# Routed layer: results scattered through three views of the output, and one gather issued earlier

## The chip, the cores and the metric

One core of one Trainium2 chip. The metric is the time of one execution on the device in microseconds (us). TensorE is called PE below, VectorE DVE, ScalarE ACT, GpSimd POOL; SP is the queue from which most loads are issued. Each engine runs its own instructions in order and waits on semaphores for the others.

## The reference

Three layers follow one another on 1152 tokens of width 512:

```python
x = attention(q, k, v)                    # 2 x 8 heads, 576 tokens, rotary positions, softmax
x = softplus(x @ w_in) @ w_out            # 512 -> 2048 -> 512
do = (x @ w_skip) > 0                     # routed layer from here
out = x.copy()
xc = x[do]
logits = xc @ w_gate                      # 8 experts
e = argmax(logits); p = softmax(logits)[e]
for each expert j: y[e == j] = p * (relu(xc[e == j] @ w1[j]) @ w2[j])   # 512 -> 1024 -> 512
out[do] = xc + y
```

The change lies in the routed layer alone.

## The kernel before

Attention and the second layer take the first part of the span. As the second layer's results come, they are written twice: to a scratch tensor in DRAM (`x2d`, a row of 512 values, a gate and a token number) and to the output, because a token that no expert takes keeps its row. That is the copy at L1489 (`out_dram<-x`, ten transfers of SP).

The routed layer then works on tiles of 128 tokens of one expert. Tile 0 is worked off in `passage`, tiles 1 to 6 in the loop of `tiles` (`range(1, FULL)`, `FULL = 7`); two "small" tiles for the remainders of several experts are woven in (`SMALL`). Tiles beyond that exist only inside conditionals, which this input doesn't enter. In `passage` PE, DVE, ACT and SP issue in the order of the text; in `tiles` all engines do, POOL too.

What a tile T needs, in order:

- `fetch(T)` (L983): POOL gathers the tile's 128 rows from `x2d` into `xg` with an indirect transfer. `small_fetch` (L1185) does it for a small tile. There are five `xg` buffers for tiles 1 to 6.
- `rows(T)` (L997): PE turns `xg` in four transposes into `xgt`; `copies` (L1010 to L1012): ACT and DVE split the result into a high and a low part.
- `split_w`: ACT rounds a chunk of weights (`ws<-raw`, L963) and DVE subtracts it for the low part (L970); 42 of each in the layer.
- `hidden_mm` (L637, `mh`), `relu`, `turn` (L1050 to L1053, `ht`, `hT`), `result_mm` (L637, `y`).
- `finish(T)`: DVE makes the row numbers `si` (L1077) and the results `yo` (L1082), and POOL writes the 128 rows to their places in the output with an indirect transfer (L1083, a scatter). `small_finish` does it for a small tile (L1166). Rows that are only padding have a number beyond the bound and are not written.

All nine scatters name the same tensor, `self.out`, and the rows that they write are known only at run time. The framework that places the semaphores therefore takes any two of them to overlap: each scatter waits until the one before it has landed. The order on POOL is tile 0, 1, 2, small 0, tile 3, 4, small 1, tile 5, 6.

In the loop, a step T multiplies the hidden layer of T and the result of T - 1, and prepares T + 1. `fetch(T + 2)` stands after the `finish` that the step carries along:

```python
                for do in done:      # in step 1: finish(0)
                    do()
                ...
            if T + 2 <= last:
                self.fetch(T + 2, xp)
```

So the gather of tile 3 (the fourth tile) is issued on POOL in step 1, behind the scatter of tile 0, and POOL's order from there is: gather 2, gather of small 0, scatter 0, gather 3, gather 4, scatter 1.

After the loop, POOL's last work is scatter 6; then a value is loaded (L1573), a branch skips the conditionals (L1574), and the engines meet at the end (L1609).

Of the kernel before, what the change touches and what calls it, by code (L numbers as in the profile page):

```python
# [9 lines left out]

F32 = mybir.dt.float32
F32R = mybir.dt.float32r
U32 = mybir.dt.uint32
# [620 lines left out]
def some(mms, n=None):  # L634

    for mm in islice(mms, n):
        mm()  # L637


class Moe2:  # L640
# [6 lines left out]
    NT, ST, SS, G = 9, 15, 8, 4  # L647
    SM = 128 // G

    def __init__(self, tc, w_skip, w_gate, w1, w2, cst, x2d, out, rp, sp):  # L650
        self.tc, self.nc = tc, tc.nc
        nc = tc.nc
        self.w1, self.w2, self.cst, self.x2d, self.out, self.rp, self.sp = w1, w2, cst, x2d, out, rp, sp
        self.w9 = rp.tile([128, 4, 9], F32, name="w9")
        nc.scalar.dma_start(self.w9[:, :, 0:8], w_gate.rearrange("(k p) e -> p k e", p=128))
        with nc.allow_non_contiguous_dma(reason="512 words once"):
            nc.scalar.dma_start(self.w9[:, :, 8:9], w_skip.rearrange("(k p o) -> p k o", p=128, o=1))
        self.oh = rp.tile([128, 9, 8], BF16, name="oh")
        self.routed = []
        self.tok = rp.tile([128, 9, 1], F32, name="tok")  # L660
        self.xg, self.w, self.reg = {}, {}, {}
        self.lg = rp.tile([128, 9, 9], F32, name="lg")
        self.m0 = rp.tile([128, 9], F16, name="m0")
        self.extra = None
        self.ohp = sp.tile([128, 9, 128], F16, name="ohp")
        self.rd = sp.tile([128, 9, 1], I32, name="rd")

# [406 lines left out]
    def finish(self, T, xg, py, xp, parts=1):  # L1074
        nc = self.nc
        si = xp.tile([128, 1], I32, name=f"si{T}", tag="si", bufs=3)
        nc.vector.tensor_add(si, xg[:, DM + 8 : DM + 9], self.e[:, T : T + 1] if T else self.e0)  # L1077
        yo = xp.tile([128, 512], F32, name=f"yo{T}", tag="yo", bufs=2)
        n = DM // parts
        for i in range(0, DM, n):  # L1080
            s = slice(i, i + n)
            nc.vector.scalar_tensor_tensor(yo[:, s], py[:, s], xg[:, DM : DM + 1], xg[:, s], op0=ALU.mult, op1=ALU.add)  # L1082
        nc.gpsimd.indirect_dma_start(  # L1083
            out=self.out, out_offset=bass.IndirectOffsetOnAxis(ap=si.bitcast(U32), axis=0),
            in_=yo, in_offset=None, bounds_check=NTOK - 1, oob_is_err=False,
        )

    def small_load(self, n, part):

        if part == 0:  # L1090
            o = self.ST + n
            self.es = self.nc.sync.value_load(self.ei[0:1, o : o + 1], min_val=0, max_val=7)
        for c in range(4):
            self.load_chunk(self.small_raw[c], self.es, 4 * part + c)
# [58 lines left out]
    def small_finish(self, n, py, xp):  # L1153
        nc, SM, G, w = self.nc, self.SM, self.G, DM // self.G
        xg, o = self.xg["s", n], self.ST + n
        si = xp.tile([128, 1], I32, name=f"ssi{n}", tag="si", bufs=3)
        nc.vector.scalar_tensor_tensor(
            si, xg[:, DM + 8 : DM + 9], float(G), self.e[:, o : o + 1], op0=ALU.mult, op1=ALU.add
        )
        yo = xp.tile([128, w], F32, name=f"syo{n}", tag="syo", bufs=1)  # L1160
        for g in range(G):
            r = slice(SM * g, SM * g + SM)
            nc.vector.scalar_tensor_tensor(
                yo[r], py[r, 0:w], xg[r, DM : DM + 1], xg[r, w * g : w * g + w], op0=ALU.mult, op1=ALU.add
            )
        nc.gpsimd.indirect_dma_start(  # L1166
            out=self.out.rearrange("n (g d) -> (n g) d", g=G),
            out_offset=bass.IndirectOffsetOnAxis(ap=si.bitcast(U32), axis=0),
            in_=yo, in_offset=None, bounds_check=G * NTOK - 1, oob_is_err=False,
        )  # L1170
# [27 lines left out]
    def tiles(self, Ts, xp, ps_x, ps_y, ps_h, ps_a, start=None, small={}):  # L1198
# [5 lines left out]
        last, done = Ts[-1], []  # L1204
# [22 lines left out]
        for T in Ts:  # L1227
            new, first = step(T, "l"), start and T == Ts[0]
            if new is not None:
                self.small_fetch(new, xp)  # L1230
                if not first:
                    self.small_load(new, 0)
            pool, tag = ps_h[T % 2]
            ph = [pool.tile([128, 512], F32, name=f"mh{T}{c}", tag=tag) for c in range(2)]
            mms = self.hidden_mm(T, st, ph)
            some(mms, 8)
            if first:
                self.load(Ts[1], 0, 1, 2, 3)
                if new is not None:
                    self.small_load(new, 0)  # L1240
            if T == Ts[1]:

                half(0)
            some(mms, 6)
            if T == Ts[1]:
                half(1)
            if T == Ts[1]:
                some(mms)
            if (n := step(T, "x")) is not None:
                sx = self.small_x(n, ps_x)  # L1250
            rows = self.rows(T + 1, ps_x) if T < last else None
            some(mms)
            if (m := step(T, "t")) is not None:
                turned = self.small_turn(m, sm[m], ps_x)
            if prev:
                for do in done:
                    do()
                done = []
                self.split_w(T - 1, 5)
                if T > Ts[1]:  # L1260
                    self.split_w(T - 1, 6, 7)
            ahead = [] if T == last else [1, 2, 3]
            if T == Ts[1]:
                st = self.relu(T, st, xp, ph)
            if T < last:
                if T != Ts[1]:
                    self.split_w(T + 1, ahead.pop(0))
                if T > Ts[1]:
                    self.split_w(T + 1, ahead.pop(0))
                if not prev:  # L1270
                    ahead.pop(0)
                    self.split_w(T + 1, 2, low=False)
                if n is not None:
                    sm[n] = self.small_copy(n, sx, xp)
                following = self.copies(T + 1, xp, rows)
            if T != Ts[1]:
                st = self.relu(T, st, xp, ph)
            if m is not None:
                sm[m] = self.small_copied(m, turned, xp)
            if T < last:  # L1280
                if not prev:
                    self.low_w(T + 1, 2)
                for do in done:
                    do()
                done = []
                if T != Ts[1]:
                    self.split_w(T + 1, *ahead)
                    ahead = []
                if not prev:
                    self.split_w(T, 4)  # L1290
            if T + 2 <= last:
                self.fetch(T + 2, xp)
            st, half = self.turn(T, st, xp, ps_x)
            if T > Ts[0] or T == last:
                mms, py = iter(()), None
                if prev:
                    py = ps_y.tile([128, 512], F32, name=f"y{T - 1}", tag="y")
                    mms = self.result_mm(T - 1, prev, py)
                for c in range(2):
                    some(mms, 6)  # L1300
                    if T == Ts[1]:
                        self.split_w(T - 1, 6 + c)
                    half(c)
                self.split_w(T + 1, *ahead)
                if T > Ts[0]:
                    self.split_w(T, 4)
                if T == last and m is not None:
                    self.small_result(m, sm[m], xp, ps_a)()
                some(mms)
                if prev:  # L1310
                    done.append(partial(self.finish, T - 1, prev[0], py, xp))
            if not first:
                self.load(T, 5)
                if T < last:
                    self.load(T + 1, 0)
                self.load(T, 6, 7)
            if T + 2 <= last:
                self.values(T + 2)
                self.load(T + 2, 1, 2, 3)
            if T < last:  # L1320
                self.load(T + 1, 4)
            if n is not None:
                sm[n] = self.small_hidden(n, sm[n], xp, ps_a)
                self.small_load(n, 1)
            if m is not None and T < last:
                done.append(self.small_result(m, sm[m], xp, ps_a))
            prev, st = st, following
# [286 lines left out]
```

## Time and profile before

| | |
|---|---|
| median of 3 runs | 496.01 us (495.57 to 496.73) |
| the profiled execution | 497.47 us |
| its span, first to last instruction | 495.7 us, granted PE clock 0.994 |
| PE busy | 471.6 us (95%) |
| DVE, ACT, POOL busy | 371.2 us (75%), 332.2 us (67%), 127.9 us (26%) |

The rows further below come from the profiled execution and count from the start of its span. A row of a timeline gives the start, the duration, the engine, the line, the operation and its tiles (buffer numbers left out), how many instructions were merged, and in brackets how long the engine had been idle and what ended that.

### The profile page before, as it was taken

The numbers are of one execution on the slowest core, as the hardware profiler recorded it, in microseconds if no ns is written. First come the engines' busy times: TensorE is split into PE (matmuls) and PEld (weight loads), VectorE is DVE, ScalarE is ACT, GpSimd is POOL, SyncE is SP. The second block draws the span as 40 slices with busy tenths as digits, with TensorE's granted clock in tenths as the row PEclk, the third lists the DMA queues.
The fourth block names the chain that finished last, engine by engine and source line by source line (L and its number), as shares of the span: only waits on it lengthen the run. The fifth ranks groups of instructions, "written<-read, shape, count | busy, mean of one in ns | idle before, by whom it ended". The sixth has DMA issues, their size and how long they took to land. (4 is left out here: it accounts for less than half of the span.)

```text
span 495.7 us, 8838 instructions
## 1 busy us (share of the span) xinstructions
PE 471.6 (95%) x3054; PEld 382.3 (77%) x3055; DVE 371.2 (75%) x699; ACT 332.2 (67%) x782; POOL 127.9 (26%) x166
## 2 busy tenths in 40 slices
PE   7999999999999999999999999999999998999992
PEld 3777777767767678999999899899897666777681
DVE  7666776688996896798989886446785786988661
ACT  1667776776777687877666785766774477867450
POOL 0966785766221300000000000001110331621011
PEclk9999999999999999999999999999999999999997
DMA  7477547457461240233334440600328352994411
GB/s 182 150 195 196 119 120 202 100 151 204 117 176 59 97 129 0 86 110 103 91 122 128 129 125 4 212 1 3 111 86 315 134 186 96 334 315 161 147 51 37
DMA packets 41509, 65.49 MB, mean 132 GB/s; under 512 B 9087, under 2 KB 23679, under 8 KB 41456
## 3 DMA queue, kind: packets, MB, share of 16 engines
q1 hardware_dynamic: 38480, 59.99, 39.9%
q0 software_dynamic: 1344, 4.20, 2.6%
q10 hardware_dynamic: 1632, 0.66, 0.6%
q8 instruction: 26, 0.43, 0.4%
q14 instruction: 27, 0.22, 0.1%
HBM read 67.32 MB, written 6.76 MB: 149 GB/s over the span
## 5 line engine op out<-in xcount | busy, mean ns | idle before, releaser
L590 PE MATMUL h<-xh,w 128*128 128x320 f32 (+2 forms) x464 | 104.2, 309 | 0.8 <-ACT rb L95 0.8
L590 PEld LDWEIGHTS h<-xh,w 128*128 128x128 f32 x464 | 78.0, 188 | 4.7 <-ACT rb L95 1.1
L628 PE MATMUL acc<-w,gh 128*128 128x512 f32 x288 | 80.6, 396 | 0.9 <-ACT gh L618 0.9
L590 PE MATMUL h<-xl,w 128*128 128x320 f32 (+2 forms) x232 | 69.2, 308 | 0.0
L269 DVE TENSOR_REDUCE m<-s 128x1 f32<-128x576 f32 x64 | 48.0, 754 | 20.5 <-PE s L260 16.9
L628 PEld LDWEIGHTS acc<-w,gh 128*128 128x128 f32 x288 | 51.8, 188 | 11.4 <-ACT gh L618 2.5
L282 ACT ACTIVATE P<-s,m 128x576 f32<-128x576 f32 x64 | 47.6, 749 | 12.5 <-DVE m L269 12.2
L970 DVE TENSOR_TENSOR ws<-raw,ws 128x1024 fp32r<-128x1024 f32 x42 | 49.4, 1221 | 6.8 <-ACT ws L963 6.1
L603 ACT ACTIVATE y<-h 128x320 f32<-128x320 f32 (+2 forms) x58 | 25.4, 438 | 41.1 <-PE h L590 39.9
L702 POOL TENSOR_SCALAR sc<-lg 128x2 f32<-128x2 f32 (+1 forms) x3 | 0.9, 294 | 201.2 <-DVE lg L685 201.2
L351 PE MATMUL t<-ct,P 128*128 128x128 f32 x288 | 45.6, 277 | 2.5 <-ACT pt L95 2.5
L628 PE MATMUL acc<-w,gl 128*128 128x512 f32 x144 | 45.9, 392 | 0.0
L260 PE MATMUL s<-ks,qs 128*128 128x288 f32 x224 | 43.7, 317 | 2.0 <-ACT P L282 1.7
L619 DVE TENSOR_TENSOR gl<-r,gh 128x256 fp32r<-128x256 f32 (+2 forms) x42 | 25.8, 614 | 26.0 <-ACT gh L618 25.8
L963 ACT CAST ws<-raw 128x1024 fp32r<-128x1024 f32 x42 | 41.8, 1050 | 4.8 <-DMA raw<-in_moe_w_dram 4.7
L590 PEld LDWEIGHTS h<-xl,w 128*128 128x128 f32 x232 | 43.2, 188 | 2.1
L351 PEld LDWEIGHTS t<-ct,P 128*128 128x128 f32 x288 | 33.6, 140 | 9.6 <-issue 3.5
L95 ACT COPY pt<-t 128x384 f32<-128x384 f32 x60 | 28.1, 480 | 18.0 <-PE t L351 17.9
L395 PE MATMUL pv<-pt,vr 128*64 128x256 f32 (+1 forms) x256 | 37.1, 412 | 0.0
L637 PE MATMUL y<-ws,hT 128*128 128x512 f32 (+1 forms) x150 | 37.0, 393 | 0.0
L260 PEld LDWEIGHTS s<-ks,qs 128*128 128x128 f32 x224 | 31.6, 189 | 6.7 <-ACT P L282 3.6
L637 PE MATMUL mh<-ws,xgT 128*128 128x512 f32 x132 | 36.6, 419 | 0.0
(305 smaller groups left out, 943.4 us busy)
## 6 DMA issues: line engine op xcount, KB each, us to landing
raw<-in_moe_w_dram SPq DMA_DIRECT2D x56, 512.0 KB
raw<-in_moe_w_in_dram SPq DMA_DIRECT2D x16, 512.0 KB
raw<-in_moe_w_out_dram SPq DMA_DIRECT2D x16, 512.0 KB
sraw<-in_moe_w_dram SPq DMA_DIRECT2D x16, 512.0 KB
ks<-kT SPq DMA_DIRECT2D x28, 288.0 KB
qs<-qT SPq DMA_DIRECT2D x28, 128.0 KB
wr<-in_moe_w_dram SPq DMA_DIRECT2D x5, 512.0 KB
x2d<-x SPq DMA_DIRECT2D x9, 256.0 KB
```

Source lines behind the costliest of these rows:

```text
L95: self.nc.scalar.copy(out, in_)
L260: nc.tensor.matmul(ps[:, c, 0:288], lhsT=qs[:, a, uc], rhs=ks[:, a, x, 288 * c : 288 * c + 288], start=x == 0, stop=x == 1,)
L269: self.last = nc.vector.tensor_reduce(st["m"][:, a : a + 1], st["ps"][a][:, :, 0:288], axis=AX.XY, op=ALU.max, negate=True)
L282: nc.scalar.activation(P[:, 576 * a : 576 * a + 576].rearrange("p (c n) -> p c n", c=2), ps[:, :, 0:288], AF.Exp, bias=m[:, a : a + 1], ac ...
L351: self.tail = nc.tensor.transpose(ps[:, 128 * i : 128 * i + 128], src, ident)
L395: nc.tensor.matmul(ps[r, 0:n], lhsT=v, rhs=pt[:, k, 0:n], start=i < 0, stop=i == 3, skip_group_check=True,)
L590: nc.tensor.matmul(ps[c][:, 0:m], lhsT=w[:, 0, x, 128 * k : 128 * k + 128], rhs=src[:, k, c0 + m * c : c0 + m * c + m], start=z == 0, stop ...
L619: self.last = nc.vector.tensor_sub(gl, r, gh.bitcast(F32))
L628: nc.tensor.matmul(acc[t], lhsT=g[x][:, 128 * j : 128 * j + 128], rhs=w[:, 1, y, :], start=f == f0 and z == 0, stop=f == f1 and z == 2,)
L637: mm()
L963: self.nc.scalar.copy(self.w[T, c][:, 0], self.raw[c] if raw is None else raw)
L970: self.nc.vector.tensor_sub(w[:, 1], self.raw[c] if raw is None else raw, w[:, 0].bitcast(F32))
```

## The change

The output is named through three views of the same memory, made once with `dram_disjoint_views(out, 3)`. The framework orders an access through the tensor itself against every view (so the copies of L1489 stay ahead of all scatters), and takes accesses through two different views to be free of overlap. `result()` hands the views out in turn, so that a scatter is ordered only against the third one before it and the sixth. No two tiles write the same token's row (a small tile writes quarter rows of tokens that no other tile has).

The gather of tile 3 moves from the end of step 1 to its beginning, behind the gather of small tile 0, ahead of scatter 0. The gathers of tiles 4 to 6 stay where they were.

```diff
+from concourse.ap import dram_disjoint_views
...
+        self.outs, self.wrote_out = dram_disjoint_views(out, 3), 0
...
         nc.gpsimd.indirect_dma_start(
-            out=self.out, out_offset=bass.IndirectOffsetOnAxis(ap=si.bitcast(U32), axis=0),
+            out=self.result(), out_offset=bass.IndirectOffsetOnAxis(ap=si.bitcast(U32), axis=0),
...
+    def result(self):
+        self.wrote_out += 1
+        return self.outs[self.wrote_out % 3]
...
-            out=self.out.rearrange("n (g d) -> (n g) d", g=G),
+            out=self.result().rearrange("n (g d) -> (n g) d", g=G),
...
                 self.small_fetch(new, xp)
                 if not first:
                     self.small_load(new, 0)
+            if first:
+                self.fetch(T + 2, xp)
             pool, tag = ps_h[T % 2]
...
-            if T + 2 <= last:
+            if T + 2 <= last and not first:
                 self.fetch(T + 2, xp)
```

## Rows read from the trace of the kernel before

**Rows 1.** Waits of PE from 398 to 487 us: total, times, longest.

```profile
PE xgt L997 <- DMA xg<-x2d,gi: 1.9, 1, 1.9
```

**Rows 2.** Busy time by window: window, length, then PE, PEld, DVE, ACT, POOL.

```profile
413.45:486.10 72.65, 72.64 (x494) 55.22 (x494) 54.80 (x69) 46.71 (x65) 17.69 (x10) 1.00 0.49 173
```

**Rows 3.** Timeline of POOL, 479 to 490 us.

```profile
480.16 1.84 POOL L1166 DMA_INDIRECT out_dram<-syo,ssi  x1 [14.32 <-DVE syo L1163]
484.97 0.98 POOL L1083 DMA_INDIRECT out_dram<-yo,si  x1 [2.97 <-DVE si L1077]
489.49 0.99 POOL L1083 DMA_INDIRECT out_dram<-yo,si  x1 [3.54 <-issue]
```

**Rows 4.** Line 1083, from 484.5 us: durations min/median/max in ns; landing in us.

```profile
L1083 POOLq EVENT_SEMAPHORE  x1: 3934/3934/3934, 484.8 to 484.8; - x1
...
DMA to landing us min/median/max: 3.8/3.8/3.8
```

**Rows 5.** Timeline of DVE, 478 to 488 us.

```profile
481.24 0.75 DVE L1082 SCALAR_TENSOR_TENSOR yo<-y,xg 128x512 f32<-128x512 f32 x1
481.91 2.35 DVE L970 TENSOR_TENSOR ws<-raw,ws 128x1024 fp32r<-128x1024 f32 x2
...
486.16 0.88 DVE L1082 SCALAR_TENSOR_TENSOR yo<-y,xg 128x256 f32<-128x256 f32 x2 [1.83 <-PE y L637]
```

**Rows 6.** Timeline of POOL, 393 to 412 us.

```profile
397.63 1.00 POOL L1185 DMA_INDIRECT sxg<-x2d,gi  x1 [0.31 <-issue]
406.31 1.97 POOL L1083 DMA_INDIRECT out_dram<-yo,si  x1 [7.68 <-DVE yo L1082]
408.58 1.03 POOL L983 DMA_INDIRECT xg<-x2d,gi  x1 [0.30 <-issue]
```

**Rows 7.** Timeline of PE, 410.9 to 420.5 us.

```profile
410.91 0.60 PE L1100 MATMUL sxt<-ct,sxg 128*128 128x128 f32 x4
413.45 0.63 PE L997 MATMUL xgt<-ct,xg 128*128 128x128 f32 x4 [1.95 <-DMA xg<-x2d,gi]
...
417.50 3.04 PE L637 MATMUL y<-ws,hT 128*128 128x512 f32 x12
```

**Rows 8.** The gather issued at 408.58 us: median us from issue to landing.

```profile
xg<-x2d,gi POOLq DMA_INDIRECT x1, 4.7
```

**Rows 9.** All seven gathers into xg: us from issue to landing.

```profile
DMA to landing us min/median/max: 3.8/4.7/6.0
```

**Rows 10.** Timeline of DVE, 393 to 409 us.

```profile
398.51 4.62 DVE L970 TENSOR_TENSOR ws<-raw,ws 128x1024 fp32r<-128x1024 f32 x4
403.61 0.56 DVE L1012 TENSOR_TENSOR xgT<-xgt,xgT 128x384 fp32r<-128x384 f32 x1 [0.48 <-ACT xgT L1011]
...
406.15 2.36 DVE L970 TENSOR_TENSOR ws<-raw,ws 128x1024 fp32r<-128x1024 f32 x2
```

**Rows 11.** Timeline of POOL, 424 to 439 us.

```profile
424.99 6.30 POOL L1083 DMA_INDIRECT out_dram<-yo,si  x1 [14.07 <-DVE yo L1082]
```

**Rows 12.** Timeline of DVE, 424 to 432 us.

```profile
424.63 5.76 DVE L970 TENSOR_TENSOR ws<-raw,ws 128x1024 fp32r<-128x1024 f32 x5
```

**Rows 13.** Timeline of DVE, 410.9 to 420.5 us.

```profile
410.33 0.69 DVE L1053 TENSOR_TENSOR hT<-ht,hT 128x512 fp32r<-128x512 f32 x1 [1.13 <-issue]
411.27 1.23 DVE L970 TENSOR_TENSOR ws<-raw,ws 128x1024 fp32r<-128x1024 f32 x1 [0.25 <-ACT ws L963]
414.86 0.56 DVE L1012 TENSOR_TENSOR xgT<-xgt,xgT 128x384 fp32r<-128x384 f32 x1 [2.36 <-ACT xgT L1011]
...
417.55 1.22 DVE L970 TENSOR_TENSOR ws<-raw,ws 128x1024 fp32r<-128x1024 f32 x1
```

**Rows 14.** Timeline of ACT, 410.9 to 420.5 us.

```profile
414.18 0.27 ACT L1010 COPY xgw<-xgt 128x128 f32<-128x128 f32 x1 [1.79 <-PE xgt L997]
```

**Rows 15.** Line 1574 on POOL's sequencer, from 490.3 us: durations min/median/max in ns.

```profile
L1574 POOLq EVENT_SEMAPHORE  x5: 17/43/2020, 490.3 to 490.7; - x5
```

**Rows 16.** All seven scatters of full tiles: us from issue to landing.

```profile
DMA to landing us min/median/max: 3.4/4.7/6.6
```

## The prediction

> **What bounds the kernel now.** I first asked the waits of PE in the last 100 us, then the windows of the same stretch, then POOL's timeline, since both edits touch only what POOL issues. PE waits for one thing between 398 and 487 us: the gathered rows of a tile, once, for 1.9 us [rows 1]. From the end of that wait to its last product PE is busy for 72.64 of 72.65 us [rows 2]. So the routed layer is PE's chain, with one hole in it; whatever closes the hole moves everything behind it, as long as nothing else is late. Behind PE's last product stands a second chain: DVE makes the last results, POOL scatters them, the scatter lands, the engines meet. There the reader is to look at POOL's idle time before the last two scatters [rows 3].
>
> **The end: three views.** The results of tile 6 are complete at 486.16 + 0.88 = 487.04 us [rows 5]. The scatter that writes them starts at 489.49, after 3.54 us of idle time that the timeline can name only as issue [rows 3]. What it waited for is in the rows of line 1083: POOL's sequencer stood in a wait of 3.93 us from 484.83 on, up to 488.76, and the scatter before, begun at 484.97, is said to land 3.8 us later, at 488.8 [rows 3, 4]. So scatter 6 waits for scatter 5 to land. Scatter 5 is late itself for the same reason: its results were there at 481.24 + 0.75 = 481.99 [rows 5] and POOL was free at 480.16 + 1.84 = 482.00, but it starts at 484.97 [rows 3]. The profile names the DVE instruction si there; that one belongs to tile 6 and isn't needed by scatter 5, so I read it as the landing of small tile 1's scatter, begun at 480.16.
>
> With the views each scatter is ordered against the third before it. For scatter 6 that is scatter 4, for scatter 5 scatter 3, both of earlier steps. Both waits go. Scatter 5 then begins at 482.00 + 0.30 = 482.3, where 0.30 is the gap that POOL leaves between two transfers that wait for nothing [rows 6]; a scatter that DVE's subtractions hold up, see below, may take until about 485.2, still ahead of the next. Scatter 6 begins at 487.04 + 0.30 = 487.34 instead of 489.49: **2.15 us**. What follows it stays: the last landing, waited for from about 490.67 for 2.02 us [rows 15], and the meeting of the engines. That puts the landing at 492.69, 3.2 us behind the scatter's start, and I keep this 3.2, since it is the same transfer on a quiet chip. The bounds are the other scatters: at the 4.7 of the middle one [rows 16] 0.65 us would be left of the gain; at the longest, 6.6, the end would lose 1.25.
>
> The seven other scatters lose waits too. That is worth nothing by itself: POOL's waits there delay no engine, because PE waits for nothing of POOL's but the one gather [rows 1].
>
> **The hole: gather 3.** PE has turned the small tile's rows at 410.91 + 0.60 and stands until 413.45, when the rows of tile 3 are there, 1.95 us of idle time [rows 7]. Their gather was issued at 408.58, directly behind scatter 0, which began at 406.31 and had waited 7.68 us for tile 0's results [rows 6]; it takes 4.7 us to land [rows 8], 3.7 of them after its issue of 1.03. After the change it is issued right behind the small tile's gather, at 397.63 + 1.00 + 0.30 = 398.9. That is one transfer moved past one scatter; nothing is added on POOL, and scatter 0 still finds POOL free if the gather is issued by 406.3. By its landing times, 3.8 to 6.0 us [rows 9], the rows would be there between 402.7 and 404.9, some 7 us before PE wants them.
>
> Its place is not as good as that, though. From 398.51 DVE subtracts weights without pause for 4.62 us [rows 10]. Scatter 1 met such a run: issued at 424.99, 0.36 us into a run of 5.76, it was done only after 6.30 us, 0.9 us behind the run's end at 430.39 [rows 11, 12]. By that row the gather's issue ends at 398.51 + 4.62 + 0.9 = 404.0 and lands 3.7 later, at 407.7. That still leaves 3.8 us before 411.5. The hole closes whole; the 3.8 us are the cover, and without them the gain goes first.
>
> The Trainium skill, page "SBUF — State Buffer", section "SBUF: two separate sides", says that GpSimd cannot write the descriptors of its transfers while DVE holds the port pair that the two share, and that it goes on about 0.1 us after DVE lets go. The 6.30 us of scatter 1 agree with the lock, the 0.9 us behind it are longer than the page's figure; by the page alone the issue would end near 403.2, and the sum stays the same. The page speaks against putting a gather here: rival A is this rule in its strict form.
>
> **What is late next.** Could PE start tile 3's transposes at 411.5? The bank they write is freed by DVE at 410.33 + 0.69 = 411.02 [rows 13], and PE's own previous work ends at 411.51: yes. ACT and DVE were waiting in the hole as well: ACT 1.79 us for the same transposes, DVE 2.36 us behind ACT [rows 13, 14], so they move along with PE. The tightest meeting I find behind the hole is the low part of the last weights of tile 1's result: DVE has it at 417.55 + 1.22 = 418.77 [rows 13], and PE, which takes it at the ninth of twelve products from 417.50, spaced 3.04/12 = 0.25, wants it at 419.5 [rows 7]. That is 0.7 us of slack. If DVE didn't move, PE would keep 0.7 of the 1.95; but the subtraction is third in a row of work that begins behind the transposes, so I take **1.95 us**, with 0.7 as the low bound. The gather moves 128 rows of 528 words, 270 KB, past the small tile's weights that are loaded then; those are first used at 417.50 + 3.04 = 420.5 [rows 7]. From there on PE has no hole to stop the gain [rows 2].
>
> **The sum.** 1.95 + 2.15 = 4.1 us off a span of 495.7, or off the profiled execution's 497.47. That execution is 1.46 us above the median of the three runs, so I take the difference off the median: 496.01 - 4.1 = **491.9 us**.
>
> **Rivals.**
> - **A, the gather starves.** If the descriptors wait not for one run of subtractions but for those behind it too, up to 406.15 + 2.36 = 408.51 [rows 10], the gather lands at 408.51 + 0.9 + 3.7 = 413.1, and 1.6 of the 1.95 us come back: 496.01 - 0.35 - 2.15 = 493.5. Against it: between the runs DVE is idle for 0.48 us and then reads PSUM (403.61), and scatter 0 got through in 1.97 us although it began inside a run of two [rows 6, 10].
> - **A', the other side: slower.** If it is held beyond the next subtraction, to 411.27 + 1.23 = 412.50 [rows 13], it lands at 412.5 + 0.9 + 3.7 = 417.1, PE stands 3.65 us longer than before, and the tail gives back 2.15: 497.5. It decides when the gather's issue ends after about 411.9, since a landing at 413.45 + 2.15 = 415.6 breaks even. That would be an issue of 13 us; the longest seen is 6.30.
> - **B, the next late operand.** PE keeps only 0.7 us of the hole, because weights for tile 1's result come when they came before: 496.01 - 0.7 - 2.15 = 493.2. For it speaks the slack of 0.7; against it that ACT and DVE stood idle for the same transposes.
> - **C, the last scatter lands late.** It starts at 487.34 but needs 4.7 us: 496.01 - 1.95 - 0.65 = 493.4. Against it: nothing else is moving then.
> - **D, the views change no wait** (the semaphores are placed as before, or another one ends as late): 496.01 - 1.95 = 494.1. **E, neither edit tells**: 496.0.
>
> **Chances.** The forecast 0.66, A 0.10, A' 0.04, B 0.07, C 0.06, D 0.03, E 0.04. I give 0.2%, 1.0 us, as the least that a measurement of this kernel tells from no change: faster 0.92 (all but A' and E), same 0.04 (E), slower 0.04 (A'). The forecast's own range is 491.2 to 492.6, from 0.7 us between the three runs before and a few tenths at either term. The range reaches up over B, C and A to 493.9, and down to 491.0.
>
> **What would show it.** Right: PE has no wait for xg between 398 and 487 us; the gather of tile 3 is issued at about 399, with an issue of some 5 us rather than 1; scatter 5 starts within 0.5 us of the end of the small scatter, scatter 6 within 0.4 us of the last yo; the span ends 6.2 us after scatter 6 begins. Wrong: the wait for xg is still there (A), a new wait of PE for ws (B), more than 4 us between the last scatter and its landing (C), or a wait of POOL's sequencer of some 4 us before scatter 6 (D).

## The result, and the profile after

The changed kernel took 493.09 us (median of seven runs, 491.82 to 493.25), the kernel before 496.73 us in the same session (seven runs, 495.57 to 499.75). The ratio is 0.9917, with a 95% interval of 0.9894 to 0.9941: faster, by 2.9 to 5.3 us. Timed again later, beside the experiments, it was 0.9934 (0.9920 to 0.9947), some 3.3 us. The interval of the first ratio is wide because the runs of before spread over 4 us, one of them at 499.75; I take 3.3 us as the better figure, and the experiments say why it isn't the 4.5 us by which the two profiled spans differ (495.7 and 491.2).

The waits of PE from 390 to 487 us, which answer to [rows 1] (line numbers have moved by three and more):

```profile
PE idx L910 <- DVE et L916: 0.3, 1, 0.3
PE idx L901 <- DVE oht L887: 0.2, 1, 0.2
PE xgt L1000 <- DMA xg<-x2d,gi: 0.2, 1, 0.2
```

The wait of 1.9 us is gone. The one of 0.2 us at 396.77 is for the rows of tile 1, whose gather the change doesn't touch. From the transposes of tile 3 to PE's end there is no hole (window, length, then busy time of PE, PEld, DVE, ACT, POOL), as in [rows 2]:

```profile
411.43:484.00 72.57, 72.57 (x496) 55.19 (x494) 55.87 (x70) 47.77 (x68) 19.85 (x10) 1.00 0.51 178
```

POOL from 396 to 412 us, to lay beside [rows 6]; PE, beside [rows 7]; and DVE, beside [rows 13]:

```profile
397.68 0.99 POOL L1192 DMA_INDIRECT sxg<-x2d,gi  x1 [0.30 <-issue]
398.98 1.70 POOL L986 DMA_INDIRECT xg<-x2d,gi  x1 [0.30 <-issue]
406.39 1.97 POOL L1086 DMA_INDIRECT out_dram<-yo,si  x1 [5.71 <-DVE yo L1085]
```

```profile
410.99 0.60 PE L1107 MATMUL sxt<-ct,sxg 128*128 128x128 f32 x4
411.43 0.60 PE L1000 MATMUL xgt<-ct,xg 128*128 128x128 f32 x4
...
415.43 3.03 PE L638 MATMUL y<-ws,hT 128*128 128x512 f32 x12
```

```profile
411.35 1.23 DVE L973 TENSOR_TENSOR ws<-raw,ws 128x1024 fp32r<-128x1024 f32 x1 [0.25 <-ACT ws L966]
413.05 0.56 DVE L1015 TENSOR_TENSOR xgT<-xgt,xgT 128x384 fp32r<-128x384 f32 x1 [0.47 <-ACT xgT L1014]
...
415.73 1.21 DVE L973 TENSOR_TENSOR ws<-raw,ws 128x1024 fp32r<-128x1024 f32 x1
```

Gather 3 is issued at 398.98 instead of 408.58, and the transposes follow the small tile's by 0.44 us (411.43 - 410.99) where they followed by 2.54. DVE moved along: the subtraction with the least slack ends at 416.94, and PE wants it at 415.43 + 8 x 0.25 = 417.4.

POOL at the end, beside [rows 3], and DVE's last results:

```profile
478.05 1.83 POOL L1173 DMA_INDIRECT out_dram<-syo,ssi  x1 [14.32 <-DVE syo L1170]
480.19 1.68 POOL L1086 DMA_INDIRECT out_dram<-yo,si  x1 [0.30 <-DVE yo L1085]
485.20 0.98 POOL L1086 DMA_INDIRECT out_dram<-yo,si  x1 [3.33 <-DVE yo L1085]
```

```profile
484.05 0.88 DVE L1085 SCALAR_TENSOR_TENSOR yo<-y,xg 128x256 f32<-128x256 f32 x2 [1.83 <-PE y L638]
```

Scatter 5 follows the small one after 0.30 us, and scatter 6 starts 0.27 us behind the last results (484.93), where it started 2.45 behind them. POOL's idle time there is now named DVE yo, which is true. The 4.5 us between the profiled spans are: DVE's last results 2.11 earlier (486.16 to 484.05), the scatter 2.18 nearer to them, and 0.21 less from its start to the end of the span (6.21 to 6.00).

### The profile page after: what moved, and what is told of

It reads as the page before. It is cut to its first block, busy times and chain, and to the rows that moved or that the text cites. A ratio compares the mean times of both kernels' runs of the same rounds, so it can differ in the third digit from the quotient of the medians.

```text
span 491.2 us, 8838 instructions
## 1 busy us (share of the span) xinstructions
PE 471.3 (96%) x3054; PEld 382.1 (78%) x3055; DVE 371.8 (76%) x699; ACT 332.3 (68%) x782; POOL 130.6 (27%) x166
## 5 line engine op out<-in xcount | busy, mean ns | idle before, releaser
L283 ACT ACTIVATE P<-s,m 128x576 f32<-128x576 f32 x64 | 47.6, 749 | 12.3 <-DVE m L270 10.7
```

The source lines that it names most:

```text
L283: nc.scalar.activation(P[:, 576 * a : 576 * a + 576].rearrange("p (c n) -> p c n", c=2), ps[:, :, 0:288], AF.Exp, bias=m[:, a : a + 1], ac ...
```

## The experiments

The experiments ran on two chips; each ratio is against the kernel before on the same chip.

**One edit at a time.** The views alone: the gather goes back to its place.

```diff
-            if first:
-                self.fetch(T + 2, xp)
...
-            if T + 2 <= last and not first:
+            if T + 2 <= last:
```

> The three views stay; the gather of tile 3 goes back behind scatter 0. Theory (two independent gains): PE stands 1.95 us for the rows of tile 3 again, the last scatter starts 0.3 us after the last results, and the time is 2.2 us below before (ratio about 0.9956). Rival (one edit carries all, the other is worth nothing because its wait moves elsewhere): either the full 4.1 us with the hole in PE closed by something else, or no gain because the end waits for the PE chain alone.

Measured: 0.9956 (0.9944 to 0.9969), 2.2 us. PE has its hole again, but it is 1.1 us long, and the profile gives it another name; the last scatter starts at 485.81, 0.27 behind the last results (484.66 + 0.88). The waits of PE from 398 us, and PE around the hole:

```profile
PE xgt L1000 <- DVE ws L973: 1.1, 1, 1.1
```

```profile
410.31 0.60 PE L1107 MATMUL sxt<-ct,sxg 128*128 128x128 f32 x4
412.00 0.63 PE L1000 MATMUL xgt<-ct,xg 128*128 128x128 f32 x4 [1.10 <-DVE ws L973]
```

The name is that of what ended last before 412.00: a subtraction of DVE from 410.67 to 411.89. The transposes don't need it. In the changed kernel they began at 411.43 while the same subtraction ran from 411.35 to 412.58. The gather, issued at 407.97, landed 3.9 us later by the trace, at 411.87; it is still what PE waits for: in all four profiles with the gather in its old place the transposes start 0.13 or 0.14 us behind the gather's landing, while the end of the subtraction lies 0.95 us ahead of them in the first profile of before and about 0.1 in the others.

The gather alone: all scatters name the one output.

```diff
-        return self.outs[self.wrote_out % 3]
+        return self.out
```

> The early gather stays; all scatters name the one output again. Theory: PE has no wait for gathered rows, the last results are ready 2.1 us earlier than before, but the last scatter still starts about 2.4 us behind them, when the scatter before has landed; the time is 2.1 us below before (ratio about 0.9958). Rival (the gain at the end needs no views, it comes with the earlier PE): the last scatter starts 0.3 us behind its results and the time is 4 us below.

Measured: 0.9976 (0.9966 to 0.9986), 1.2 us and not 2.1. No hole after 398 us. The end is as expected, though the wait is shorter than 2.4 us: the last results at 483.38 + 0.88 = 484.26, the scatter 2.05 us behind them. POOL's rows name the cause for scatter 5 here, as before they didn't:

```profile
481.18 1.15 POOL L1086 DMA_INDIRECT out_dram<-yo,si  x1 [1.97 <-DMA out_dram<-syo,ssi]
486.31 0.98 POOL L1086 DMA_INDIRECT out_dram<-yo,si  x1 [3.98 <-issue]
```

The parts add up within the noise: 0.44% and 0.24% make 0.68%, the whole gave 0.66% and 0.83% in other sessions and, in the two versions of it that ran on the chip of the parts (below), 0.64% and 0.56%. But the gather's part is smaller than the hole of 1.95 us that the prediction read.

**How long is the hole?** The kernel before was profiled twice more.

> The kernel before, profiled a second time, for the size of the hole. Theory: the hole is as long as the slowest of the gather's 16 completions is late, which differs from execution to execution; with the landing of 3.9 us that the run with the views alone showed it is 1.1 us, not 1.95. Rival: the hole is 1.95 us each time, and the views made it smaller. The last scatter starts 2.4 us behind its results either way.

> The kernel before, profiled a third time. Theory (the hole depends on the slowest of the gather's completions): a hole of about 1.1 us as in two of the three profiles that have it, or longer by as much as one completion is late. Rival: 1.95 us is the rule.

Measured: 496.43 and 496.37 us, against 497.47 of the first profiled execution; spans of 494.7 and 494.6, against 495.7. The hole is 1.1 us in both. From the third profile, PE around the hole, the landing of gather 3, and POOL and DVE at the end:

```profile
411.15 0.60 PE L1100 MATMUL sxt<-ct,sxg 128*128 128x128 f32 x4
412.82 0.63 PE L997 MATMUL xgt<-ct,xg 128*128 128x128 f32 x4 [1.06 <-DVE ws L970]
```

```profile
xg<-x2d,gi POOLq DMA_INDIRECT x1, 3.9
```

```profile
484.13 0.98 POOL L1083 DMA_INDIRECT out_dram<-yo,si  x1 [2.77 <-DVE si L1077]
488.51 0.98 POOL L1083 DMA_INDIRECT out_dram<-yo,si  x1 [3.39 <-issue]
```

```profile
485.52 0.88 DVE L1082 SCALAR_TENSOR_TENSOR yo<-y,xg 128x256 f32<-128x256 f32 x2 [1.83 <-PE y L637]
```

The gather was issued at 408.82 here, and landed after 3.9 us, not 4.7. A transfer counts as landed when the last of 16 completions has come; in the trace of the first profile 15 of the gather's had come after 3.97 us and the last after 4.74, while in the other two all 16 had come by 3.89 and 3.86. So the first profile showed a hole with a straggler in it, one completion that came late. The wait at the end was longer in it too: behind the last results scatter 6 started after 2.45 us in the first profile, but after 2.14 and 2.11 in the others (488.51 - 485.52 - 0.88). Of these 0.3 us about half is that scatter 5 landed after 3.8 us in the first and 3.6 in both others, and the rest that scatter 5 itself began 0.1 to 0.2 us later against the last results. A late last completion is no accident of the first profile here: in all three, 15 of scatter 5's 16 completions had come after 2.74 us and the last came after 3.76, 3.57 and 3.61. In the change, where scatter 5 follows the small one at once, its last two came after 3.41 and 3.43. And the landing is what scatter 6 waits for: in the three profiles of before and with the early gather alone it starts 0.75 or 0.76 us behind scatter 5's last completion.

**How much of the order has to go?** Two views in turn, and then two of which only the last scatter takes the second.

```diff
-        self.outs, self.wrote_out = dram_disjoint_views(out, 3), 0
+        self.outs, self.wrote_out = dram_disjoint_views(out, 2), 0
...
-        return self.outs[self.wrote_out % 3]
+        return self.outs[self.wrote_out % 2]                    # two views
+        return self.outs[1 if self.wrote_out == 9 else 0]       # the last alone
```

> The change with two views in turn instead of three, so each scatter is ordered against the second before it. Theory: the last scatter then waits for the second small tile's scatter, which has landed about 2 us before the last results, so the profile and the time are those of the change within 0.3 us. Rival (the third view is needed): the last scatter starts up to 1 us or more behind its results.

Measured: 0.9936 (0.9922 to 0.9950), span 490.5. The last scatter starts at 484.35, 0.28 behind the last results. The third view is worth nothing here.

> The change with two views, of which only the last scatter takes the second; the eight before it stay in one chain. Theory: one edge carries the whole gain at the end, so scatter 5 starts about 2.7 us later than in the change, still before the last results, and scatter 6 starts 0.3 us behind its results; the time is that of the change. Rival (two scatters under way hinder each other): the last scatter starts or lands 0.5 to 1.5 us later than in the change, because scatter 5 is still landing.

Measured: 0.9944 (0.9930 to 0.9959), span 491.2. POOL at the end:

```profile
481.87 1.16 POOL L1086 DMA_INDIRECT out_dram<-yo,si  x1 [1.96 <-DMA out_dram<-syo,ssi]
485.22 0.98 POOL L1086 DMA_INDIRECT out_dram<-yo,si  x1 [2.20 <-DVE yo L1085]
```

Scatter 5 waits for the small one again, but scatter 6 starts 0.27 us behind its results (484.07 + 0.88 = 484.95), with scatter 5 still under way: the trace has its last completion 4.72 us after its start, at 486.6, and that of scatter 6 after 2.97. The whole gain at the end hangs on one edge of the order. Scatter 5 starts 1.7 us later than in the change (481.87 against 480.19), not 2.7. Scatter 6 isn't hindered by the scatter still under way: in the change timed again, where scatter 5 has landed before, scatter 6 lands after 2.98 us.

**The change again, and two steps further.**

> The change itself once more, to be timed beside the next two. From the two parts alone (0.9956 and 0.9976) the theory that they add up gives 0.993; the trace of before, taken at its word, gives 0.9917. In the profile: no wait of PE for the rows of tile 3, the last scatter 0.3 us behind the last results.

Measured: 0.9934 (0.9920 to 0.9947), as the sum of the parts. No hole at tile 3; the last scatter 0.27 us behind the results.

```diff
             if first:
-                self.fetch(T + 2, xp)
+                for t in (3, 4, 5):
+                    self.fetch(t, xp)
...
-            if T + 2 <= last and not first:
+            if T + 2 <= last and (not start or T == 4):
                 self.fetch(T + 2, xp)
```

> The change, with the gathers of tiles 4 and 5 moved to the same place as well. Theory: no engine waits for those, so PE's chain and the time stay (within 0.3 us of the change); the issues and transfers only stand earlier. Rival: three gathers in a row hold POOL and the transfers of the small tile's weights, and something behind them comes later, 0.5 us or more.

Measured: 0.9926 (0.9911 to 0.9941), not to be told from the change. No new wait. POOL:

```profile
398.55 1.58 POOL L986 DMA_INDIRECT xg<-x2d,gi  x1 [0.30 <-issue]
400.44 1.97 POOL L986 DMA_INDIRECT xg<-x2d,gi  x1 [0.31 <-issue]
402.71 1.00 POOL L986 DMA_INDIRECT xg<-x2d,gi  x1 [0.30 <-issue]
```

```diff
-        py = pool.tile([128, 512], F32, name=f"y{T}", tag=tag)
-        some(self.result_mm(T, prev, py, halves=(3,)))
+        py = [pool.tile([128, 512], F32, name=f"y{T}{i}", tag=tag) for i in range(2)]
+        self.result_banks(T, prev, py)     # same products, 256 columns each, left half in py[0], right in py[1];
+                                           # the last chunk: all of the left half, then all of the right
```

> The change, and the last tile's result gathered in two banks of PSUM, its left and its right half, so that DVE can finish the left half while PE still works on the right one (the same products, all in halves of 256 columns). Theory: one of DVE's two last operations, 0.4 to 0.5 us, goes under PE's work; the last scatter starts 0.75 us behind PE's end instead of 1.2, and the time is 0.4 us below that of the change, less than the timing can tell but plain in the profile. Rival: the products in halves cost PE as much as is won, or DVE waits for PE's end as before.

Measured: 0.9923 (0.9909 to 0.9937), against 0.9934 of the change on the same chip: the intervals overlap. The profile tells more. DVE's last two operations, no longer one behind the other:

```profile
483.52 0.48 DVE L1099 SCALAR_TENSOR_TENSOR yo<-y,xg 128x256 f32<-128x256 f32 x1 [1.18 <-PE y L1085]
484.22 0.48 DVE L1099 SCALAR_TENSOR_TENSOR yo<-y,xg 128x256 f32<-128x256 f32 x1 [0.22 <-PE y L1085]
```

From PE's first product of the last result the scatter starts after 9.51 us (475.47 to 484.98), in the change after 9.86 (475.78 to 485.64): 0.35 us won. PE itself takes as long as before, 8.75 us from 475.47 to DVE's second half against 8.71 to its first. The span is 491.2 against 491.7, part of which is drift ahead of this layer. It has the shortest end of the study, by an amount that the timing can't tell; the medians of this version (492.85), of the one with three gathers early (492.79) and of the change (493.23) are not to be told apart.

**What holds POOL's issue?** The prediction had gather 3 held for some 5 us by DVE's subtractions; it took 1.70, and scatter 1 again 6.29. POOL's row of scatter 1 in the change, and DVE's rows of the two runs of subtractions that gather 3 and scatter 1 met:

```profile
423.10 6.29 POOL L1086 DMA_INDIRECT out_dram<-yo,si  x1 [13.40 <-DVE yo L1085]
```

```profile
398.59 4.62 DVE L973 TENSOR_TENSOR ws<-raw,ws 128x1024 fp32r<-128x1024 f32 x4
...
422.73 5.75 DVE L973 TENSOR_TENSOR ws<-raw,ws 128x1024 fp32r<-128x1024 f32 x5
```

A small operation of DVE that reads results of PE in PSUM was put into the run that holds scatter 1.

```diff
+        self.y_last = py                  # in finish(): the results that it reads
...
                 self.split_w(T - 1, 5)
+                if start and T == 3:      # second run: two lines further down, behind split_w(T - 1, 6, 7)
+                    scr = xp.tile([128, 256], F32, name="scr", tag="scr", bufs=1)
+                    self.nc.vector.tensor_copy(scr, self.y_last[:, 0:256])
                 if T > Ts[1]:
                     self.split_w(T - 1, 6, 7)
```

> The change, and a small extra operation of DVE that reads PSUM (256 columns, its result unused) between the first and the second of the five subtractions during which scatter 1 is issued. Theory of the prediction (an issue of POOL that meets such a run waits for the run's end): the run now ends behind its first subtraction, and scatter 1 is issued in about 2 us instead of 6.3. Rival (the run isn't what holds it; the gather in the change got through at a boundary between two subtractions): the issue stays near 6.3 us.

Measured: 1.75 us. The held time passed to the next one in POOL's order; DVE's rows beside it:

```profile
423.23 1.75 POOL L1087 DMA_INDIRECT out_dram<-yo,si  x1 [13.41 <-DVE yo L1086]
425.28 4.57 POOL L986 DMA_INDIRECT xg<-x2d,gi  x1 [0.30 <-issue]
```

```profile
424.00 0.42 DVE L1272 COPY scr<-y 128x256 f32<-128x256 f32 x1
424.33 4.62 DVE L973 TENSOR_TENSOR ws<-raw,ws 128x1024 fp32r<-128x1024 f32 x4
```

> The same extra operation, behind the third of the five subtractions. Theory: scatter 1 is issued until 0.9 us behind the third subtraction's end, in about 4.1 us. Rival: 6.3 us again, or about 2 us as with the break behind the first.

Measured: 4.03 us, and 2.30 for the gather behind it:

```profile
422.81 4.03 POOL L1087 DMA_INDIRECT out_dram<-yo,si  x1 [13.42 <-DVE yo L1086]
427.15 2.30 POOL L986 DMA_INDIRECT xg<-x2d,gi  x1 [0.30 <-issue]
```

```profile
422.45 3.48 DVE L973 TENSOR_TENSOR ws<-raw,ws 128x1024 fp32r<-128x1024 f32 x3
425.86 0.41 DVE L1274 COPY scr<-y 128x256 f32<-128x256 f32 x1
426.19 2.35 DVE L973 TENSOR_TENSOR ws<-raw,ws 128x1024 fp32r<-128x1024 f32 x2
```

Each issue ends 0.9 us behind the run that it met: 422.81 + 4.03 = 426.84 against 425.93, 427.15 + 2.30 = 429.45 against 428.54; in the run before, 425.28 + 4.57 = 429.85 against 428.95. So in this stretch the run is what holds it, and where it is broken the issue goes on. That the operation in between has to read PSUM was not tried. Both kernels took about what the change takes (493.5 and 492.9 us in one run each), and PE has no wait in either from 398 us on: nobody waits for these transfers.

## Why the prediction was right, and where it was off

**The mechanism of the end** was right. The wait of POOL's sequencer was for the landing of the scatter before: with one edge taken away (the last scatter alone in its view) it was gone, with the early gather alone it stayed, at 2.05 us. That DVE's si was only a name is supported too: with the early gather alone the same place bears the name of the small scatter's landing. The size was off: the prediction took 2.15 us, and the two further profiles of before put it at 2.14 - 0.27 = 1.87 and 1.84. A later start and a slower landing of scatter 5 were in the one profile that the sum was made from. The prediction's bounds are weaker than they look: [rows 9] and [rows 16] say seven, but the trace tells the landing of five of the gathers and of four of the scatters. Scatter 1 is not among them; in the two further profiles it landed after 10.7 and 10.8 us, well beyond the 6.6 that the prediction calls the longest. This didn't matter for the last scatter, which landed after 2.97 to 3.50 us wherever the trace tells it.

**The mechanism of the hole** was right, and so was that the gain would pass through ACT and DVE to the end of PE's chain: counted from the small tile's transposes in the two profiles it came out whole, 2.10 us at the transposes of tile 3 (2.54 - 0.44) and 2.19 at DVE's last results (75.25 - 73.06). The term was mis-sized. It took 1.95 us, a hole that a straggler had made longer; the other three profiles with the gather in its old place have 1.1. Counted from start to start, the transposes of the kernel before come 1.69 and 1.67 us behind the small tile's, against 0.44, so 1.25 and 1.23 us were to be had as a rule. The gather alone was timed at 1.2.

**The sum.** With the sizes of the two further profiles it is 1.24 + 1.86 = 3.1 us, against the 3.3 us of the change timed again and the forecast of 4.1. The prediction saw that its profiled execution was 1.46 us above the median of the runs, and set this aside as an offset of both kernels. The two further profiled executions lie 1.04 and 1.10 us below the first, and the two waits together are 1.16 and 1.21 us shorter in them (2.10 and 2.18 against 1.25 and 1.87, 1.23 and 1.84): as far as three profiles show, most of the offset was late landings, in the very waits that the change removes. This is the step that failed. The time, 493.09, came out inside the whole range of 491.0 to 493.9, but outside the forecast's own 491.2 to 492.6, where the prediction had B (493.2), C (493.4) and A (493.5); the time alone would not have told the forecast from them, and the profile did. Of the 1.2 us by which it lies above the forecast, 0.7 is that the kernel before had a median of 496.73 over seven runs, of which the three that the prediction knew gave 496.01. That the first ratio, 0.9917, amounts to just the 4.1 us of the forecast is luck: it owes half a microsecond to the one run of before at 499.75.

**Gather 3's own cost** was over-estimated: an issue of 1.70 us and rows there at about 403, not 5 us and 407.7. It cost the sum nothing, because the cover of 3.8 us had been enough even for the worse case.

**The rivals.** A and A' (the gather starves): not here, its issue took 1.58 to 1.98 us in all the kernels with the gather in its new place. The danger they describe is real in the stretch from 422 us on, where the gather behind scatter 1 took 4.57 us once the run was broken in front of it. B (the next late operand): no; the slack was there, 0.5 us of it left. C (a late last landing): no; the trace has it after 2.99 us. D and E: no.

## What to carry to other kernels

When several indirect writes name one tensor, look at how long POOL idles before the last one and whether that ends with the landing of the one before; where no engine waits for the earlier ones, only the edge in front of the last write is worth anything, and one disjoint view for it did the same here as three in turn. This is open only to writes that really never touch the same row. A wait that ends with a transfer's landing has no fixed length: before it is priced from one profile, compare that execution's time with the other runs, and if it is slow, suspect the landing and take a second profile. A gather that an engine waits for should be issued as soon as its list of rows is there and not behind a scatter that waits for results, with several us of cover for an issue that may be held.

## What the runs showed of the hardware

In the stretch from 422 us, a transfer issued by POOL while DVE subtracts weights from SBUF into SBUF (128x1024, 1.22 us each, one directly behind the other) was held until DVE turned to an operation that reads PSUM. Unhindered, such an issue takes 1.0 us. Five issues of the change and of the two kernels with the broken run ended 0.9 us behind the end of the run, whether it was of one, two, three, four or five subtractions. The Trainium skill, page "SBUF — State Buffer", section "SBUF: two separate sides", describes a lock on ports that DVE and POOL share, held for a whole instruction. It names operations of DVE in a two-port mode and, only where POOL's instruction reads SBUF, those with two inputs in SBUF; the subtraction has two such inputs, and the transfers take their row numbers from tiles in SBUF (`gi`, `si`), but no run shows that this is why. The trace agrees that POOL waits, but its 0.9 us behind the run's end are more than the page's 0.1, which was measured with a copy, and in this stretch POOL didn't get in between two instructions either.

Elsewhere it did. Gather 3 of the change, issued 0.39 us into the first of four subtractions, ended at 400.68, 0.87 us behind that first one (398.59 + 1.22), with three more to come; five other issues of the change (scatter 0, the first small scatter, gather 6, scatters 3 and 5, of 1.68 to 2.02 us) and, with three gathers early, gather 4 (1.97 us) got through in the same way, ending 0.85 to 0.95 us behind one subtraction while the next still ran. So of the issues that met several subtractions in the change, only scatter 1 was held to the end of the run. What distinguishes its stretch is not settled: the subtractions follow each other as closely in both, and no run changed that alone.

Of the same transfer in repeated executions the slowest of 16 completions came up to 0.9 us later in one than in the others (gather 3 of the kernel before: 4.74, 3.89 and 3.86 us), with no edit between them. Why is open.
